# Attention into SwiGLU on one core: the third batch's score steps at closer slots, and the second batch's first P V in one step of four banks

## The chip, the cores and the metric

The kernel runs on one core of a Trainium2 chip. The metric is the device time of one execution in microseconds (us); several executions are timed and their median is taken. One more execution is profiled, and all rows and durations below come from it.

The core has TensorE (PE, with its weight loads listed apart as PEld), VectorE (DVE), ScalarE (ACT), GpSimd (POOL) and SyncE (SP), each with its own queue of instructions that it works through in order. Matmuls write into PSUM, which has eight banks of 128 x 512 fp32; ScalarE and VectorE read them from there.

## The reference

```python
# 8 batches, 8 heads, 1024 positions, head size 64, projection 64
k_proj = np.einsum('ks,bhsd->bhkd', E, k)
v_proj = np.einsum('ks,bhsd->bhkd', F, v)
scores = scale * np.matmul(q, k_proj.transpose(0, 1, 3, 2))
attn = softmax(scores)                       # over the 64 projected keys
attn_out = np.matmul(attn, v_proj)
x = attn_out.transpose(0, 2, 1, 3).reshape(8192, 512)
g = x @ w_gate                               # 512 x 1536
out = (silu(g) * (x @ w_val)) @ w_out        # 1536 x 512
```

Inputs and output are fp32, and the matmuls work in bf16.

## The kernel before

**Chunks and iterations.** A batch is cut into two halves ("ch") of 512 positions, which makes 16 chunks `c`. The feed-forward part of a chunk needs its attention output `xT[b, ch]` (four tiles of 128 features by 512 positions). The main loop runs over 16 x 12 = 192 iterations `t`; iteration t does feature block f = t mod 12 of chunk c = t div 12: four gate matmuls (`f_g`, line 493, PSUM tile `gps`), four value matmuls (`f_v`, line 499, tile `vps`), both of 512 columns. ScalarE takes Tanh of the gate (line 496), VectorE makes s and then the hidden tile `hT` (lines 503 and 508) from it and the value. "g" and "v" have two PSUM banks each, so a gate or value matmul group needs the bank of the group two before it to have been read.

The output matmuls of the chunk before (`f_m`, line 626; for chunk 0 `f_y`, line 514) are placed behind the value matmuls, by a table `late`. From chunk 1 on they are done in a form with seven half-size products instead of eight, for which GpSimd and VectorE make sums of hidden quarters (`hs`, line 569), and the parts are put together at lines 602 to 625 with the banks "y" and "z" (one each).

**Slots.** All attention work of the following batches is put by hand between these groups. Iteration t has the slots 2t (after its gate matmuls) and 2t + 1 (after its value matmuls and output matmuls). `put(s, fn, ...)` files a step under a slot, `run_slot(s)` calls what is there; this sets the order in which each engine's instructions are issued. Loads of a slot go first. `place(b)` (line 681) holds the slots of batch b; s0 = 48 (b - 1). Batches count from 0 in the code: the second batch is b = 1, the third is b = 2.

**The steps of one batch.**

- `u_TD` (line 327): a transposing DMA of the queries, issued by SP, one for each half.
- `u_KV`, `u_K1`, `u_V1`, `u_KT`: projections of k and v, and the block-diagonal `BD` that the scores are multiplied with. `VS` holds the projected values.
- `u_S` (line 343): one score step, four matmuls of 128 columns (line 353) into one "a" bank, and one Exp on ScalarE (line 357). A half has four, a batch eight (`sa[0]` to `sa[7]`).
- `u_R` (line 365) in the slot after it: sum and reciprocal on VectorE (lines 368 and 370).
- `u_N` (line 373) in the same slot: the product with the reciprocal on GpSimd (line 383), into `AAd`, a tile for one half.
- `u_AD` (line 335): the turn of a half, a transposing DMA from `AAd` to `AT` (line 337), issued by SP. It needs all four products of its half. For the third batch on it stands four slots behind the fourth and the eighth score step.
- `u_PVt` (line 419): P V of a half. Each group g does four matmuls of 64 x 64 (line 430) into two PSUM banks; then the banks are copied to `xT` by ScalarE (line 439), last group first. It waits for `AT`. The argument `gs` says which of the two groups, and `ats` from which pools each group's two banks come.

**Banks.** "a" has two banks. While the loop is in chunks 0 and 1, each request for "a" is served in rotation from three banks:

```python
if where == "a" and ring["wide"]:
    where = "aaz"[ring["n"] % 3]
    ring["n"] += 1
```

From chunk 2 on (slot 48) "a" means its own two banks.

**Queues.** SP issues all transposing DMAs and the stores of the output, in the order of the program. GpSimd issues the loads of k, v and q between its own products; for the fourth batch (b = 3) they stand at slots 76, 78, 80 and 82. The query turns of the fourth batch are put at slots 90 and 92. Up to eight banks, two `AT`, two `AAd` and two `qTd` tiles are shared by all batches.

Of the kernel before, what the change touches and what calls it, by code (L numbers as in the profile page):

```python
# [38 lines left out]
def kernel(  # L39
# [638 lines left out]
    def put(s, fn, *a):  # L678
        slots[s].append((fn, a))

    def place(b):
        s0 = 48 * (b - 1)
        if b == 1:
            put(22, u_TD, 1, 0)
            put(29, u_K1, 1)
            put(32, u_KT, 1)
            put(40, u_V1, 1)
            sa = (35, 36, 37, 38, 41, 42, 43, 44)
            put(41, u_AD, 1, 0)
            put(30, u_TD, 1, 1)  # L690
            put(47, u_AD, 1, 1)
            put(45, u_PVt, 1, 0, (0,), ("aa", "aa"))
            put(46, u_PVt, 1, 0, (1,), ("aa", "aa"))
        else:
            if b == 2:
                put(s0 + 10, u_KV, b)
            else:
                put(s0 + 8, u_KV, b, "kv", (0, H), "v")
            put(s0 + (13 if b == 2 else 11), u_KT, b)
            put(s0 + (9 if b == 2 else -6), u_TD, b, 0)  # L700
            put(s0 + (11 if b == 2 else -4), u_TD, b, 1)
            sa = [s0 + j for j in ((17, 22, 24, 27, 30, 33, 36, 39) if b == 2 else (14, 17, 20, 23, 26, 29, 32, 35))]
            put(sa[3] + 4, u_AD, b, 0)
            put(sa[7] + 4, u_AD, b, 1)
            put(s0 + 44, u_PVt, b, 0, (0, 1), ("aa", "yz"))
        for j in range(NJ):
            put(sa[j], u_S, b, j)
            put(sa[j] + 1, u_R, b, j)
            put(sa[j] + 1, u_N, b, j)
        put(s0 + (68 if b == 1 else 56), u_PVt, b, 1, (0, 1), ("aa", "yz"))  # L710
# [5 lines left out]
    with tc.manual_schedule():  # L716
# [129 lines left out]
        for b in range(1, B):  # L846
            place(b)
        for b in range(2, B):
            s0 = 48 * (b - 1) - (20 if b == 3 else 24)
# [71 lines left out]
```

## Time and profile before

| what | value |
| --- | --- |
| median of 3 runs | 549.01 us (548.2 to 549.5) |
| the profiled execution's own time | 548.17 us |
| its span in the profile | 546.4 us, so 1.77 us lie around it |
| granted TensorE clock, mean | 1.00 of full speed |
| busy: PE / DVE / POOL / ACT | 98% / 75% / 54% / 43% of the span |
| one iteration of the loop, third batch on | about 2.7 us (the k and v projections start at 159.06 and 223.91, 24 iterations apart) |
| score step: PE / ACT / DVE / POOL | 0.22 / 0.60 / 0.68 + 0.20 / 1.05 us |
| turn of `AAd` to `AT`, issue to landing (14) | least 4.3, median 13.7, greatest 19.7 us |
| third batch's score steps start on PE | 106.06, 113.23, 115.83, 119.96, 123.43, 128.21, 131.67, 135.80 us |
| third batch's turns issued by SP | 124.19 and 148.21 us |
| fourth batch's loads issued by GpSimd | k 122.15, v 124.10, q 129.22 and 131.40 us |
| P V: second batch / third batch | 77.35 and 78.66, 109.62 / 142.83, 158.43 us |

Times in the rows are counted from the start of the span. A matmul's end in the trace is modelled and overlaps the next one, so lengths on PE are best read from the start of one group to the start of the next: a group of four 512-column matmuls takes 0.86 us that way, though each is shown with 0.38. "idle before" in brackets is the time that the engine had nothing running in front of a row, with what released it. The share of busy time is an average; what a stage is limited by is read from the rows of that stage.

### The profile page before, as it was taken

To read this page: it belongs to the slowest core of one execution; us is meant where nothing else is said; L and a number is where in the kernel's file an instruction comes from. 1 tells how busy PE (TensorE), PEld (TensorE's weight loads), DVE (VectorE), ACT (ScalarE), POOL (GpSimd) and SP (SyncE) were. 2 spreads that over 40 slices of the span, in tenths; PEclk is the share of its full clock that TensorE was granted. 3 is DMA by queue.
4 is the path that set the end of the run, shared out by engine and by line. 5 is a ranking of instruction groups with operands and counts; after the bars stand their busy time and mean duration, and the time that the engine had idled before them with its cause. 6 is when DMAs were issued, how large, how long until landed. Compare 5 with 4: busy or idle time off the path is not lost.

```text
span 546.4 us, 9372 instructions
## 1 busy us (share of the span) xinstructions
PE 534.6 (98%) x3494; PEld 313.6 (57%) x3556; DVE 412.5 (75%) x697; ACT 233.2 (43%) x416; POOL 294.6 (54%) x364
## 2 busy tenths in 40 slices
PE   8999999999999999999999999999999999999997
PEld 4654445556555665566555665556655565556565
DVE  3787897779578886788777886787967888676884
ACT  3664443354444334444344444434344433443331
POOL 6952493466616854168641875338660665426162
PEclk9999999999999999999999999999999999999999
DMA  9999979919941499018990099612993133110013
GB/s 203 189 196 189 166 153 192 169 40 146 212 106 40 91 184 215 13 39 132 191 180 38 29 154 201 121 40 51 170 200 82 39 78 79 38 40 9 30 40 117
DMA packets 111630, 62.88 MB, mean 115 GB/s; under 512 B 65888, under 2 KB 102752, under 8 KB 111584
## 3 DMA queue, kind: packets, MB, share of 16 engines
q0 software_dynamic: 43952, 29.49, 38.0%
q1 hardware_dynamic: 66800, 31.20, 27.0%
q10 hardware_dynamic: 832, 1.57, 0.9%
q8 instruction: 28, 0.46, 0.4%
q14 instruction: 18, 0.15, 0.1%
HBM read 60.29 MB, written 16.78 MB: 141 GB/s over the span
## 4 chain that ended last, share of the span: by engine, by line
PE 84%; DMA 12%; POOL 2%; issue 1%; ACT 0%; DVE 0%; POOLq 0%; DVEq 0%; ACTq 0%
PE vps L484 26%; PE gps L484 26%; PE yps L586 24%; DMA qTd<-qb 3%; DMA AT<-AAd 3%; PE sc L353 2%; DMA qb<-in_q_dram 2%; PE kvp L163 2%; PE pv L430 2%; DMA Fraw<-in_F_dram 1%; PE yps L520 1%; DMA wv<-in_moe_w_val_dram 1%; POOL wv L127 0%; POOL AA L383 0%; POOL wg L127 0%
## 5 line engine op out<-in xcount | busy, mean ns | idle before, releaser
L496 ACT ACTIVATE th<-gps 128x512 f32<-128x512 f32 x191 | 114.3, 598 | 197.3 <-PE gps L484 177.9
L484 PE MATMUL vps<-xT,wv 128*128 128x512 bf16 (+1 forms) x754 | 195.3, 377 | 0.9
L484 PE MATMUL gps<-xT,wg 128*128 128x512 bf16 (+1 forms) x734 | 192.4, 377 | 1.3
L503 DVE SCALAR_TENSOR_TENSOR s<-th,gps 128x512 f32<-128x512 f32 x191 | 129.3, 677 | 61.3 <-ACT th L496 59.9
L508 DVE SCALAR_TENSOR_TENSOR hT<-s,vps 128x512 bf16<-128x512 f32 x192 | 132.0, 688 | 22.6 <-PE vps L484 2.5
L569 POOL TENSOR_TENSOR hs<-hT 128x256 bf16<-128x256 bf16 x180 | 120.4, 692 | 48.7 <-DVE hT L508 48.6
L484 PEld LDWEIGHTS <-wv 128*128 128x128 bf16 x776 | 73.1, 98 | 84.6 <-issue 6.5
L586 PEld LDWEIGHTS <-hs 128*128 128x128 bf16 x900 | 88.0, 98 | 34.7 <-issue 0.6
L484 PEld LDWEIGHTS <-wg 128*128 128x128 bf16 x776 | 73.9, 98 | 51.6 <-issue 0.4
L616 POOL TENSOR_TENSOR tt<-tt,ysb 128x512 f32<-128x512 f32 x28 | 35.6, 1271 | 111.4 <-DVE tt L615 111.4
L383 POOL TENSOR_TENSOR AAd<-ee,rr 128x512 bf16<-128x512 f32 x56 | 58.5, 1046 | 34.5 <-DVE rr L370 28.9
L586 PE MATMUL yps<-ws,hs 128*128 128x256 bf16 x540 | 68.6, 273 | 0.2 <-DVE ysb L653 0.2
L357 ACT ACTIVATE ee<-sc 128x512 f32<-128x512 f32 x64 | 37.9, 596 | 30.7 <-PE sc L353 29.4
L605 POOL TENSOR_TENSOR tt<-xs 128x256 f32<-128x256 f32 x30 | 29.6, 987 | 37.5 <-ACT xs L603 37.0
L586 PE MATMUL yps<-ws,hT 128*128 128x256 bf16 x360 | 48.8, 273 | 0.3
L586 PE MATMUL yps<-wo,hs 128*128 128x256 bf16 x360 | 48.6, 273 | 0.1
L368 DVE TENSOR_REDUCE zz<-ee 128x8 f32<-128x512 f32 x64 | 43.3, 677 | 5.6 <-ACT ee L357 5.4
L569 DVE TENSOR_TENSOR hs<-hT 128x1536 bf16<-128x1536 bf16 (+1 forms) x49 | 45.3, 929 | 0.1
L586 PEld LDWEIGHTS <-hT 128*128 128x128 bf16 x360 | 35.2, 98 | 16.0
L439 ACT CAST xT<-pv 128x512 bf16<-128x512 f32 x56 | 28.9, 601 | 2.3 <-PE pv L430 2.3
L603 ACT COPY xs<-yps 128x512 f32<-128x512 f32 x30 | 17.6, 587 | 27.9 <-PE yps L586 24.6
L610 ACT COPY ysb<-yps 128x512 f32<-128x512 f32 x30 | 17.6, 587 | 27.7 <-PE yps L586 22.9
(100 smaller groups left out, 306.5 us busy)
## 6 DMA issues: line engine op xcount, KB each, us to landing
out_dram<-ysb SPq DMA_DIRECT2D x28, 512.0 KB, 2.7
qb<-in_q_dram POOLq DMA_DIRECT2D x14, 512.0 KB, 18.6
kb<-in_k_dram POOLq DMA_DIRECT2D x7, 1024.0 KB, 10.9
vb<-in_v_dram POOLq DMA_DIRECT2D x7, 1024.0 KB, 15.8
wo<-in_moe_w_out_dram POOLq DMA_DIRECT2D x2, 768.0 KB, 21.5
out_dram<-ysb SPq DMA_DIRECT2D x6, 256.0 KB, 2.3
kraw<-in_k_dram ACTq DMA_DIRECT2D x2, 512.0 KB, 5.0
qb<-in_q_dram POOLq DMA_DIRECT2D x4, 256.0 KB, 7.8
```

Of the source, the lines that this page charges most:

```text
L357: nc.scalar.activation(out=e[:].rearrange("p h j k -> p (h j k)"), in_=ps[:].rearrange("p a k -> p (a k)"), func=AF.Exp, scale=scale,)
L368: nc.vector.reduce_sum(out=z[:], in_=e[:], axis=AX.X)
L383: eng.tensor_tensor(out=a.rearrange("p j h k -> p h j k"), in0=ee.pop((b, u))[:], in1=rr.pop((b, u))[:].unsqueeze(3).to_broadcast([P, 4, 2 ...
L439: nc.scalar.copy(out=xT[b, ch][:, kt, :], in_=ps[:])
L484: nc.tensor.matmul(out=ps[:, ts], lhsT=(wg, wv)[w][:, kt, f * P : (f + 1) * P], rhs=x[:, kt, ts], start=(kt == 0), stop=(kt == NKT - 1),)
L496: nc.scalar.activation(out=th[:], in_=ps[:], func=AF.Tanh, scale=0.5)
L503: nc.vector.scalar_tensor_tensor(out=s1[:], in0=th[:], scalar=1.0, in1=g[:], op0=ALU.add, op1=ALU.mult)
L508: nc.vector.scalar_tensor_tensor(out=hT[c][:, f, :], in0=s1[:], scalar=0.5, in1=ps[:], op0=ALU.mult, op1=ALU.mult)
L569: eng.tensor_tensor(out=hs[c, m][:, fs, :], in0=quarter(hT[c], *a)[:, fs], in1=quarter(hT[c], *b)[:, fs], op=op,)
L586: nc.tensor.matmul(out=ps, lhsT=lhsT, rhs=ws[m][:, f, :] if rhs is None else rhs, start=(start and f == 0), stop=(f == HF - 1), skip_group ...
L605: nc.gpsimd.tensor_tensor(out=t[:, 0], in0=xs[:, 0], in1=xs[:, 1], op=ALU.add)
L616: nc.gpsimd.tensor_tensor(out=t[:], in0=t[:], in1=yo[c, p][:, 1:3], op=ALU.subtract)
```

## The change

Two places of `place(b)` differ.

```diff
@@ place(b), b == 1
-            put(45, u_PVt, 1, 0, (0,), ("aa", "aa"))
-            put(46, u_PVt, 1, 0, (1,), ("aa", "aa"))
+            put(46, u_PVt, 1, 0, (0, 1), ("aa", "av"))
@@ place(b), b >= 2
-            sa = [s0 + j for j in ((17, 22, 24, 27, 30, 33, 36, 39) if b == 2 else (14, 17, 20, 23, 26, 29, 32, 35))]
+            sa = [s0 + j for j in ((17, 18, 22, 23, 27, 30, 33, 36) if b == 2 else (14, 17, 20, 23, 26, 29, 32, 35))]
             put(sa[3] + 4, u_AD, b, 0)
             put(sa[7] + 4, u_AD, b, 1)
```

In the second batch's first half, P V was done in two steps: group 0 at slot 45 (behind iteration 22's value and output matmuls) and group 1 at slot 46 (behind iteration 23's gate matmuls), each into two banks of the rotation and each followed by two copies. Now both groups are one step at slot 46: eight matmuls into four banks, three of the rotation and one of "v", then four copies. The rotation is advanced by three instead of four.

In the third batch (s0 = 48) the eight score steps go from slots 65, 70, 72, 75, 78, 81, 84, 87 to 65, 66, 70, 71, 75, 78, 81, 84, and their sums, reciprocals and products with them, each one slot behind. The turn of the first half goes from slot 79 to 75, that of the second half from 91 to 88, which is ahead of the fourth batch's query turn at slot 90 and not behind it any more. P V of the third batch stays at slots 92 and 104. All other batches and steps are as before.

## The prediction

> **What bounds the kernel now.** I read the page first: shares of the span by engine, then waits, chain, and the timeline around the slots that the change names.
>
> ```profile
> PE 534.6 (98%) x3494; PEld 313.6 (57%) x3556; DVE 412.5 (75%) x697; ACT 233.2 (43%) x416; POOL 294.6 (54%) x364
> ...
> PE pv L430 <- DMA AT<-AAd: 1.0, 1, 1.0
> ```
>
> TensorE (PE) is busy 98% of the span. Of all its named waits, one lies behind the start-up and is worth a microsecond: P V waits once for a transpose. So an edit pays if it shortens PE's own sequence or removes this wait. The chain of waits between 118 and 150 us shows the wait:
>
> ```profile
> 124.19 18.59 DMA AT<-AAd
> 142.78 0.04 issue
> 142.83 0.63 PE pv L430 x8
> ```
>
> It is the third batch's first half: the transpose is issued at 124.19, lands 18.59 us later, and P V (slot 92) starts at that moment. Next the timeline of PE at the second batch's P V (slots 45 and 46):
>
> ```profile
> 76.40 0.81 PE L520 MATMUL yps<-wo,hT 128*128 128x512 bf16 x3
> 77.35 0.41 PE L430 MATMUL pv<-AT,VS 64*64 64x512 bf16 x4
> 77.70 1.04 PE L484 MATMUL gps<-xT,wg 128*128 128x512 bf16 x4
> 78.66 0.71 PE L430 MATMUL pv<-AT,VS 64*64 64x512 bf16 x4
> 79.30 1.04 PE L484 MATMUL vps<-xT,wv 128*128 128x512 bf16 x4
> 80.18 1.89 PE L520 MATMUL yps<-wo,hT 128*128 128x512 bf16 x8
> 81.90 1.03 PE L484 MATMUL gps<-xT,wg 128*128 128x512 bf16 x4
> ```
>
> In the same stretch the weight loads (PEld) and ScalarE's copies, from the timeline of all engines:
>
> ```profile
> 77.84 1.07 ACT L439 CAST xT<-pv 128x512 bf16<-128x512 f32 x2 [1.24 <-PE pv L430]
> ...
> 78.66 0.11 PEld L430 LDWEIGHTS <-VS 64*64 64x64 bf16 x3 [0.42 <-issue]
> ...
> 78.97 0.10 PEld L430 LDWEIGHTS <-VS 64*64 64x64 bf16 x1 [0.20 <-issue]
> ```
>
> And slot 68, where the same function does both halves of its work in one step:
>
> ```profile
> 108.67 1.03 PE L484 MATMUL gps<-xT,wg 128*128 128x512 bf16 x4
> 109.62 0.63 PE L430 MATMUL pv<-AT,VS 64*64 64x512 bf16 x8
> 110.18 1.04 PE L484 MATMUL vps<-xT,wv 128*128 128x512 bf16 x3
> ...
> 110.30 2.06 ACT L439 CAST xT<-pv 128x512 bf16<-128x512 f32 x4
> ```
>
> Columns: start, duration, engine, line, operation. Durations overlap, so I count from start to start: four 512-wide matmuls take 0.86 us (the chain's pieces of four, and 81.90 to the next group at 82.77; single records are missing, so x3 stands for four too). The reader is to see the pause inside the second step (the fourth weight load comes at 78.97, as the first step's copies end at 77.84 + 1.07 = 78.91), and that eight matmuls in one step have no such pause.
>
> **Part 1, one step of four banks at slot 46.** Start to start, the first small step costs 77.70 - (76.40 + 0.86) = 0.44 us, the second 79.30 - (77.70 + 0.86) = 0.74 us, together 1.18. The single step at 109.62 costs 110.18 - (108.67 + 0.86) = 0.65 us. Gain: 0.53 us. Its two pieces: 0.74 - 0.44 = 0.30 us is the second step's wait for the first bank's copy (three banks in rotation, the fourth allocation meets the first again; the new fourth bank is one of "v"), and 1.18 - 0.30 - 0.65 = 0.23 us is one pair of changes between 128x128 and 64x64 matmuls. The Trainium skill, "TensorEngine Tiling (Array Packing)", Key Properties, says that a change of tiling mode drains TensorE. By that rule alone one step instead of two would be worth the 0.23 us and no more; the rows show 0.53, and I follow the rows.
>
> What the step has to meet. (a) Its "v" bank was last read by hT of two iterations earlier, long done; the value matmul of iteration 23 now takes the bank of iteration 22, whose hT runs 77.26 to 77.95. New times: gate 77.26, P V 78.21, value 78.77. Free by 0.8 us. (b) ScalarE: Tanh of iteration 23 starts 1.07 to 1.10 us after its gate, so 78.35, ends 78.95; four copies take 2.06, so the last ends at 81.0. The gate of the next chunk reads all four; PE arrives at 81.90 - 0.53 = 81.37. Cover 0.37 us. Were it gone, each microsecond of lateness costs one. The next readers of ScalarE's queue (a copy of y, then Tanh) had over a microsecond of idle time in front of them. (c) Transposed AT of this half was issued at 70.47, 4.7 us to landing: no issue. I take 0.53; bounds 0 (the copies late by all of it) and 0.60.
>
> **Part 2, scores at 17, 18, 22, 23, 27, 30, 33, 36 instead of 17, 22, 24, 27, 30, 33, 36, 39.** As sets, two positions change: the score step of slot 87 moves to 66 and that of 72 to 71; the other six positions stay and carry a different part. Nothing is added: eight score steps of 0.22 us on PE, eight Exp of 0.60, eight reductions (0.68 + 0.20) on VectorE (DVE), eight products of 1.05 on GpSimd (POOL). The first turn needs four products, so it now follows slot 72, not 76. Computed: PE is at -0.53 from part 1 and +0.22 from the extra score step, so the step of slot 71 ends at about 114.9, its Exp at 115.7. DVE reduces slot 70 till 116.65, slot 71 till 117.55; the product ends at 118.8. The turn is issued there, against 124.19: 5.4 us earlier. SP's only earlier entry is the output at 116.20, done in 0.4.
>
> What the turn then takes: this tile's times from issue to landing are 4.3 / 13.7 / 19.7 us (least, median, greatest). The short ones are those without loads beside them, and the DMA engines are idle from about 119.0 to 123.5 now, until the third load of k (issued at 122.15) begins. Near 124 is my estimate; even with 19.7 it is 138.5. P V wants it at 140.78 + 0.95 - 0.53 = 141.2 (0.95 is gate to P V at 108.67). So the wait is gone with 2.7 us left in the worst row. Its size, start to start: 142.83 - (140.78 + 0.95) = 1.10 us (the list's 1.0 counts from a modelled end). That is the second term; bounds 0 and 1.10.
>
> Costs of the move, each with its cover. PE runs 0.22 us later from slot 66 to 87, then it is returned. DVE: the reduction of slot 67 falls into the 0.90 us in which s waits for Tanh at 110.36; that of slot 72 puts 0.88 ahead of s of iteration 36, so its hT ends near 119.1, where value matmuls that want this bank start near 120.7; the next s finds its reduction already done. Without cover it would be 0.88 us. ScalarE: the Exp of slot 66 ends near 108.0, ahead of the copy that frees the "y" bank for P V of slot 68; that copy starts with PE (108.87 now) and not with Exp. POOL: one more product near 111, where it has 2.36 us idle before 113.20; the loads of k, v and q keep their places behind the same other work. The score step of slot 71 takes a bank whose copy ended by 112.4. All at nothing.
>
> SP's queue: the second turn (AD of slot 88, was 91) is now ahead of both query transposes of the fourth batch, where it stood between them. It can be issued at about 135.8 instead of 148.21, into the running loads. Behind it in the queue stand the two query transposes, issued at 145.16 and 151.34 now (the first waits for its load anyway), wanted by the scores at 168.8. An issue beside loads has held SP for up to 9.53 us: 135.8 + 9.5 = 145.3, no later than now. P V of the second half is at 158.43, new 156.8: it waits if this turn takes over 21 us.
>
> **Sum.** 546.40 (span) - 0.53 - 1.10 = 544.8; with the 1.77 us around it, 548.17 becomes 546.5. The profiled execution is the lowest of the runs shown (548.2, 549.0, 549.5); on their median 549.01 - 1.63 = 547.4. I predict the median.
>
> **Rivals.**
> A. Only the transpose wait goes; the four copies hold the next chunk's gate and return part 1. For it: ScalarE must do 2.06 us in a row with 0.37 to spare. Against: slot 68 runs the very same sequence in the time used. 549.0 - 1.1 = 547.9; with part of it, 547.4 to 547.9.
> B. Only part 1 is gained: the turn is held up on POOL or DVE, or lands behind the loads, and P V waits as before. 549.0 - 0.5 = 548.5. Against: 5.4 us of lead where 1.1 is needed.
> C. Slower: the second turn, now in the middle of the loads, lands after 156.8, and P V of slot 104 is the new wait, with all later work behind it. It decides from 21.0 us on; above 23.7 us both gains and 1.1 us more are gone: 550.1. The greatest of 14 turns is 19.7. For it: it is issued with 3 MB of loads in flight, as the 18.59 us turn was. Against: the loads' last packets are over near 147.6 now, and it can finish then.
> The skill's "SBUF — State Buffer", Who interferes with whom, speaks against more GpSimd work here: a DVE instruction with two SBUF inputs and a GpSimd one that reads SBUF block each other. The row agrees: hs on DVE takes 1.28 us at 123.71 beside a product, else 0.95. By that rule a moved product may cost DVE 0.33 us, and PE nothing as long as DVE's idle time stands; no such hs lies beside the two moved products.
>
> **Chances.** Forecast (both gains) 0.68, A 0.13, B 0.13, C and other losses 0.06. No change means within 0.2%, 1.1 us, which is about what a measurement of this kernel can tell. The forecast itself is 1.6 below the median and runs spread by about 0.7 to each side, so some of it falls within no change, as does most of B and half of A: faster 0.70, same 0.24, slower 0.06. Range: 546.2 (1.63 and 1.2 of spread to the lower side) to 548.6 (case B).
>
> **What would show it.** One group of eight P V matmuls near 78.2 with no pause in the weight loads; value matmuls 0.56 us behind; the next chunk's gate at 81.4 without ScalarE as its releaser. Turn issued near 119, landed before 130; no wait of P V for AT in the list; P V of slot 92 at 141.2 and everything after it 1.6 us earlier. Wrong if a wait of PE for AT appears at slot 104, or for a query transpose near 167, or if the copies end after 81.4.

## The result and the profile after

| | before | changed |
| --- | --- | --- |
| median (6 runs each) | 548.43 us (548.06 to 549.5) | 546.64 us (546.45 to 547.08) |
| ratio, 95% interval | | 0.9966 [0.9953, 0.9978] |
| profiled execution: own time / span | 548.17 / 546.4 us | 546.79 / 545.0 us |

The changed kernel is 1.79 us faster; the interval leaves 1.2 to 2.6 us. That is under 2%, but the whole interval lies beyond the 0.2% within which the prediction speaks of no change.

First the second batch's P V, in the timeline of PE, to be laid beside the rows from 76.40 to 81.90 of before:

```profile
77.52 1.03 PE L484 MATMUL gps<-xT,wg 128*128 128x512 bf16 x4
78.47 0.63 PE L430 MATMUL pv<-AT,VS 64*64 64x512 bf16 x8
79.03 1.04 PE L484 MATMUL vps<-xT,wv 128*128 128x512 bf16 x4
79.91 1.89 PE L520 MATMUL yps<-wo,hT 128*128 128x512 bf16 x8
81.63 1.03 PE L484 MATMUL gps<-xT,wg 128*128 128x512 bf16 x4
```

There is one group of eight. From the gate group's start to the value group's start there are 79.03 - 77.52 = 1.51 us, as at slot 68 before. The output group ahead of all this begins 0.25 us later than before (76.65 against 76.40: this execution's start-up was slower), while the gate of the next chunk comes 0.27 us earlier (81.63 against 81.90). Part 1 gave 0.25 + 0.27 = 0.52 us.

The timeline of all engines shows the cover, ScalarE's copies:

```profile
79.15 2.05 ACT L439 CAST xT<-pv 128x512 bf16<-128x512 f32 x4
```

They end at 81.20, the gate that reads them starts at 81.63. The cover is 0.43 us and holds.

The third batch's first turn, in SP's timeline and then with its time to landing in the DMA view of 119 to 120 us:

```profile
116.16 0.38 SPq L622 DMA_DIRECT2D out_dram<-ysb  x1
119.14 1.67 SPq L337 DMA_TRANSPOSE AT<-AAd  x1
132.55 0.37 SPq L622 DMA_DIRECT2D out_dram<-ysb  x1
136.33 5.49 SPq L337 DMA_TRANSPOSE AT<-AAd  x1
143.10 7.39 SPq L330 DMA_TRANSPOSE qTd<-qb  x2
```

```profile
AT<-AAd SPq DMA_TRANSPOSE x1, 4.2
```

It is issued 5 us earlier and lands after 4.2 us instead of 18.6, so at 123.3; P V needs it at 141.5. PE at slot 92 no longer waits. First the timeline of before, then that of the changed kernel:

```profile
140.78 1.03 PE L484 MATMUL gps<-xT,wg 128*128 128x512 bf16 x4
142.83 0.63 PE L430 MATMUL pv<-AT,VS 64*64 64x512 bf16 x8 [1.02 <-DMA AT<-AAd]
143.38 1.04 PE L484 MATMUL vps<-xT,wv 128*128 128x512 bf16 x3
```

```profile
140.51 1.03 PE L484 MATMUL gps<-xT,wg 128*128 128x512 bf16 x4
141.47 0.63 PE L430 MATMUL pv<-AT,VS 64*64 64x512 bf16 x8
142.03 1.04 PE L484 MATMUL vps<-xT,wv 128*128 128x512 bf16 x3
```

Gate to P V is 0.96 us, against 2.05 before (142.83 - 140.78): 1.09 us gained. On the way there the moved score steps cost PE nothing: the gate group at 140.51 is 0.27 us earlier than before (140.78), just as the gate of chunk 2 was (81.63 against 81.90). The value group stands at 142.03 against 143.38, 1.35 us earlier, and that is where it stays: the projections of the fourth batch start 1.36 us earlier (157.70 in the chain, 159.06 before), the span ends 1.4 us earlier. No later wait takes anything back. 0.52 + 1.09 less the 0.25 of the start-up makes 1.36.

### The profile page after: what moved, and what is told of

It is laid out like the page before. It is cut to its first block, busy times and chain, and to the rows that moved or that the text cites. A ratio compares the mean times of both kernels' runs of the same rounds, so it can differ in the third digit from the quotient of the medians.

```text
span 545.0 us, 9374 instructions
## 1 busy us (share of the span) xinstructions
PE 534.2 (98%) x3494; PEld 313.4 (58%) x3556; DVE 412.8 (76%) x697; ACT 232.8 (43%) x416; POOL 294.2 (54%) x364
## 4 chain that ended last, share of the span: by engine, by line
PE 88%; DMA 8%; POOL 2%; issue 1%; ACT 0%; DVE 0%; POOLq 0%; DVEq 0%; ACTq 0%
PE vps L484 28%; PE gps L484 27%; PE yps L586 25%; DMA qTd<-qb 3%; PE sc L353 3%; DMA qb<-in_q_dram 2%; PE kvp L163 2%; DMA Fraw<-in_F_dram 1%; PE pv L430 1%; PE yps L520 1%; DMA wv<-in_moe_w_val_dram 1%; POOL wv L127 0%; POOL AA L383 0%; POOL wg L127 0%; POOL qb L117 0%
```

## The experiments

All ran beside the kernel before on the same chip, in three sets, and medians are compared within a set. The kernel before took 548.42 us in the first (28 runs, e1 to e4), 548.32 in the second (26, e5 to e7) and 548.45 in the third (10, e8 to e10).

**e1: part 1 alone.**

```diff
-            put(45, u_PVt, 1, 0, (0,), ("aa", "aa"))
-            put(46, u_PVt, 1, 0, (1,), ("aa", "aa"))
+            put(46, u_PVt, 1, 0, (0, 1), ("aa", "av"))
```

> Part 1 alone (P V of the second batch's first half in one step at slot 46; scores and turns of the third batch as before). Theory (two independent terms): TensorE gains 0.53 us at slots 45 and 46 and the wait of P V for AT at slot 92 stays at 1.1 us, so about 0.5 us below the kernel before. Rival (the two parts work together, or the gain of part 1 is given back at the AT wait, which then grows by what PE arrives earlier): no change, with a wait of about 1.6 us.

Measured 548.01 us, ratio 0.9993 [0.9981, 1.0004]: 0.4 us below, not clear of no change by the time alone. The trace is clearer. The step has the form of the changed kernel (gate 77.52, P V 78.48, value 79.04), and the AT wait is still there:

```profile
140.52 1.03 PE L484 MATMUL gps<-xT,wg 128*128 128x512 bf16 x4
142.53 0.63 PE L430 MATMUL pv<-AT,VS 64*64 64x512 bf16 x8 [0.98 <-DMA AT<-AAd]
```

142.53 - 140.52 - 0.95 = 1.06 us, not 1.6. PE arrives earlier, but so does the whole chain of scores, products, turn and loads that PE sets going (turn issued at 123.93, 18.6 us to landing). The rival falls.

**e2: part 2 alone.**

```diff
-... (17, 22, 24, 27, 30, 33, 36, 39) if b == 2 ...
+... (17, 18, 22, 23, 27, 30, 33, 36) if b == 2 ...
```

> Part 2 alone (closer score steps and earlier turns; P V of the second batch's first half in two steps as before). Theory: the AT wait at slot 92 is gone, 1.1 us below the kernel before, with the pause in the second small P V step still there. Rival (the closer steps cost something on DVE, ScalarE or GpSimd that part 1 hides): less than 0.8 us below.

Measured 547.30 us, ratio 0.9979 [0.9969, 0.9989]: 1.1 us below, as expected. The interval leaves 0.6 to 1.7 us, so the time alone does not exclude the rival's 0.8; the trace does. The first turn is issued at 119.45 and takes 4.2 us; gate to P V at slot 92 is 141.78 - 140.83 = 0.95. And PE loses nothing between the two places: the gate of chunk 2 is 0.05 us later than in the kernel before (81.95 against 81.90), and the gate of slot 92 is too (140.83 against 140.78). Together e1 and e2 make 1.5 of the 1.8 us, within what such medians allow; the parts add up.

**e3: what part 1 is made of.** Two steps as before, and one letter changed:

```diff
-            put(46, u_PVt, 1, 0, (1,), ("aa", "aa"))
+            put(46, u_PVt, 1, 0, (1,), ("aa", "av"))
```

> The kernel before with one letter changed: the second small P V step at slot 46 takes its fourth bank from v and not from the rotation; still two steps. It splits part 1. Theory: the bank wait of 0.30 us goes (no pause before the fourth weight load of that step), the second pair of tiling changes stays: value matmuls 0.44 us behind the end of the gate group, 0.3 us below the kernel before, not to be told from no change by the time alone; the trace decides. Rival (the pause is not the bank): the pause stays and 0.74 us too.

Measured 548.33 us, ratio 0.9997 [0.9987, 1.0008]: nothing to be seen in the time. The weight loads in its timeline decide:

```profile
77.53 0.11 PEld L430 LDWEIGHTS <-VS 64*64 64x64 bf16 x4 [0.42 <-issue]
77.88 0.55 PEld L484 LDWEIGHTS <-wg 128*128 128x128 bf16 x4 [0.23 <-issue]
78.84 0.11 PEld L430 LDWEIGHTS <-VS 64*64 64x64 bf16 x4 [0.42 <-issue]
79.19 0.55 PEld L484 LDWEIGHTS <-wv 128*128 128x128 bf16 x4 [0.23 <-issue]
```

The second step's four loads now come together, with no pause before the fourth. Its price is 79.19 - (77.88 + 0.86) = 0.45 us, that of the first 0.44. So the pause was the bank, 0.29 us, and the remaining 0.45 + 0.44 - 0.65 = 0.24 us of part 1 is one pair of tiling changes. It is not the price of any step put in between: a score step, four matmuls of 128 columns in the 128x128 form, costs 0.22 us, which is what 512 columns take (0.86 / 4). The idle times of the loader at each entry (0.42) and exit (0.23) fit what the Trainium skill's "TensorEngine Tiling (Array Packing)", Key Properties, says of a change of mode: TensorE drains. The rows agree with the rule, but it would have found less than half of the gain; the loader's idle 0.65 us is also not its price to PE, which is 0.24.

**e4: the turns back in their old slots,** the rest as in the changed kernel.

```diff
-            put(sa[3] + 4, u_AD, b, 0)
-            put(sa[7] + 4, u_AD, b, 1)
+            put(s0 + 31 if b == 2 else sa[3] + 4, u_AD, b, 0)
+            put(s0 + 43 if b == 2 else sa[7] + 4, u_AD, b, 1)
```

> The changed kernel with only the turns of the third batch put back to slots 79 and 91; scores stay close, P V in one step. Theory: the turn is issued by SP as soon as the fourth product is done (near 119 us), whatever its slot, since no other entry of SP stands in between; same time as the changed kernel, 546.6. Rival (the slot of the turn is what counts): the turn is issued near 124 again, and P V waits 1 us at slot 92: 547.7.

Measured 546.99 us, 1.4 us below the kernel before, ratio 0.9965 [0.9951, 0.9979], close to the changed kernel's 0.9966. P V of slot 92 does not wait (gate 140.10, P V 141.06). SP's timeline:

```profile
118.73 1.67 SPq L337 DMA_TRANSPOSE AT<-AAd  x1
132.15 0.37 SPq L622 DMA_DIRECT2D out_dram<-ysb  x1
141.41 3.01 SPq L330 DMA_TRANSPOSE qTd<-qb  x1
144.51 1.90 SPq L337 DMA_TRANSPOSE AT<-AAd  x1
```

The turn is issued when its fourth product is done. Its slot only matters for its place in SP's queue, which for the first turn is the same; the second one waits behind a query turn again (144.51, not 136.33) and nobody notices, as P V of slot 104 comes at 156.67. It is the score steps that brought the gain.

**e5: the kernel before, with the fourth batch's loads put later** instead of the scores earlier. The second turn goes to slot 89, so that it does not stand behind a query turn.

```diff
-            s0 = 48 * (b - 1) - (20 if b == 3 else 24)
+            s0 = 48 * (b - 1) - (16 if b == 3 else 24)
...
-            put(sa[7] + 4, u_AD, b, 1)
+            put(sa[7] + (2 if b == 2 else 4), u_AD, b, 1)
```

> The kernel before with the loads of the fourth batch four slots later (80, 82, 84, 86), and the second turn of the third batch at slot 89, so that it does not stand behind a query transpose that waits for these loads. Scores, the first turn (slot 79) and both small P V steps as before. Theory (the turn lands late because the loads share the DMA engines with it): issued near 124 as before, it lands in 4 to 7 us, P V at slot 92 does not wait, 1.1 us below the kernel before. Rival (the late issue itself is the cause): it lands 15 us or more after its issue again and the wait stays.

Measured 547.39 us, ratio 0.9985 [0.9973, 0.9998]: 0.9 us below; the near end of the interval is only 0.1 us from no change, so the trace decides. The turn in SP's timeline, its time to landing in the DMA view of 123 to 125 us, and the k load in GpSimd's timeline:

```profile
123.91 1.69 SPq L337 DMA_TRANSPOSE AT<-AAd  x1
```

```profile
AT<-AAd SPq DMA_TRANSPOSE x1, 4.3
```

```profile
129.12 0.94 POOL L98 DMA_DIRECT2D kb<-in_k_dram  x1
```

The turn is issued 0.28 us from where it was, lands in 4.3 us, and the k load comes behind it. Gate to P V is 141.99 - 141.03 = 0.96, no wait. The late turn was slow because of the loads beside it, and not because it was late.

**e6: the cover taken away.**

```diff
-            put(46, u_PVt, 1, 0, (0, 1), ("aa", "av"))
+            put(47, u_PVt, 1, 0, (0, 1), ("aa", "av"))
```

> The changed kernel with the one-step P V of the second batch's first half at slot 47, right ahead of the gate group that reads its result, and not at 46. It takes away the cover of the four copies. Theory: P V start to last copy is 2.73 us, P V start to the next group 0.56 us, so the gate of chunk 2 waits about 2.2 us for ScalarE: 548.8, about as much above the changed kernel. Rival (the copies are hidden by something else, or the first copies suffice): under 1 us above it.

Measured 549.12 us, ratio 1.0022 [1.0012, 1.0033], 0.8 us above the kernel before. Against that less the changed kernel's 1.79 us it is 2.6 us more. PE's timeline:

```profile
81.31 0.63 PE L430 MATMUL pv<-AT,VS 64*64 64x512 bf16 x8
84.09 1.02 PE L484 MATMUL gps<-xT,wg 128*128 128x512 bf16 x4 [2.16 <-ACT xT L439]
```

2.78 us instead of 0.56: a wait of 2.2 us, as worked out. The two profiles differ by the same amount: the span is 2.5 us longer (547.5 against 545.0), of which 0.25 us lay ahead of this place (output group at 76.90 against 76.65). One slot too late turns the gain of the whole change into a loss; at slot 46 there are 0.43 us to spare.

**e7: half the lead.** Score steps at 17, 22, 23, 24, 27, 30, 33, 36.

```diff
-... (17, 18, 22, 23, 27, 30, 33, 36) if b == 2 ...
+... (17, 22, 23, 24, 27, 30, 33, 36) if b == 2 ...
```

> The changed kernel with less lead: third batch's score steps at 17, 22, 23, 24, 27, 30, 33, 36, so that the first turn follows the step of slot 72 and is issued near 121.5, just ahead of the fourth batch's k load, not near 119. Theory (what counts is to be in front of the loads): it lands in under 10 us, no wait at slot 92, same as the changed kernel within 0.2%. Rival (the lead of 5 us counts as such; a landing is 18 us when loads follow): it lands near 140 and P V has under 1.5 us left or waits.

Measured 547.05 us, ratio 0.9975 [0.9965, 0.9985], 1.3 us below the kernel before; whether it is as good as the changed kernel these intervals don't say. The profiled execution was its slowest (548.7 us), late from the start: its first query turn was issued at 42.78 and not 41.15. The rows at slot 92 are counted from one another and can be read all the same. SP issues the turn and GpSimd the k load:

```profile
122.57 1.69 SPq L337 DMA_TRANSPOSE AT<-AAd  x1
```

```profile
123.19 0.94 POOL L98 DMA_DIRECT2D kb<-in_k_dram  x1
```

Landing takes 7.7 us, and gate to P V is 143.35 - 142.40 = 0.95: what the theory says, and not the rival's landing near 140. With e2, e5 and the kernels before and after this makes a row by the distance of the turn from the issue of the k load:

| turn issued | issue to landing |
| --- | --- |
| 5.2 us before the k load (e5) | 4.3 us |
| 3.0 us before it (changed, e2) | 4.2 us |
| 0.6 us before it (e7) | 7.7 us |
| 2.0 us after it (before) | 18.6 us |

From the third line to the fourth are 2.6 us of distance and 10.9 us of landing time. The k load is not all that differs between these two: in the kernel before, the v load too was issued ahead of the turn (124.10 against 124.19), in e7 it came 3.5 us behind it (126.03). SP issues the turn and GpSimd the loads; the skill's "DMA: Bandwidth & Descriptors", section "Issuing engines are not separate DMA queues", says that DMAs of both run on the same 16 DMA engines and interleave. The table agrees in so far as a turn on SP's queue is slow when GpSimd's loads run beside it.

**e8, e9 and the changed kernel again.** In the profile after, the one PE wait for a transpose that is left is the second batch's first score step, at 59.94, behind a query turn that takes 18.7 us among the loads of the start. Two kernels try the same cure there.

```diff
-        put(20, load_v, 1)
+        put(25, load_v, 1)
```

> The changed kernel with the same idea used at the start: the second batch's load of v at slot 25 and not 20, so that fewer loads run beside the first query turn (issued at 41.15, 18.7 us to landing, and PE waits for it at 59.9 in the changed kernel's profile). Theory (a turn among loads is slow, wherever it is): the turn lands some microseconds sooner, the wait of 0.2 to 0.5 us goes: 0.3 us below the changed kernel. Rival (v then lands too late for its projection at slot 40, or its wait only moves): no gain, or slower, with a wait of PE for v near 68.

```diff
-            sa = (35, 36, 37, 38, 41, 42, 43, 44)
+            sa = (36, 37, 38, 39, 41, 42, 43, 44)
```

> The changed kernel with the second batch's first four score steps one slot later (36, 37, 38, 39 and not 35 to 38), so that PE has a gate group to do while the first query turn lands. Theory: the wait near 59.9 goes (0.2 to 0.5 us), and the first turn of this batch, then about 1 us later, still lands before P V at slot 46: 0.3 us below the changed kernel. Rival (the turn gets late): P V at slot 46 waits for AT, no gain.

> The changed kernel unaltered, beside the two others on one chip, as their measure. Theory and rivals alike: 1.4 to 1.9 us below the kernel before.

Measured: e8 546.76 us, 0.9969 [0.9956, 0.9981]; e9 546.40 us, 0.9966 [0.9953, 0.9978]; the changed kernel 546.72 us, 0.9969 [0.9957, 0.9981]. e8 brings nothing, and it has hardly tested its idea, as GpSimd's timeline shows:

```profile
42.84 0.94 POOL L117 DMA_DIRECT2D qb<-in_q_dram  x1
43.77 0.88 POOL L108 DMA_DIRECT2D vb<-in_v_dram  x1
```

GpSimd has no product between the two slots that would hold the load back, so v only changed places with the second load of q: v was issued at 43.77 and not at 42.31, q at 42.84 and not at 43.25. Both still run beside the turn, with k until 46.5 and the second load of the output weights until 57.1. The turn takes 17.7 us, one less; PE does not wait for it in this profile, but PE also comes 0.5 us later there (output group at 58.21 and not at 57.69). Whether a load of v that is really later would help stays open. In e9's profile the wait is gone, and P V at slot 46 doesn't wait either; its median is 0.3 us lower, and the intervals can't tell that from none. In the profile of e10 PE loses only 0.1 us at this place (output group at 57.50, eight matmuls of 0.216, first score at 59.35), where the first profile of the changed kernel lost 0.5 (57.69 to 59.94); the query turn was issued at 40.59 there, 0.56 us earlier. So this wait grows and shrinks with the start-up. None of the three is shown to be better than the others.

## Why the prediction was right

1. *Bound: PE's sequence and one wait.* Right. Each of the two terms moved everything behind it by its full size, and the end with it.
2. *Part 1, 0.53 us.* 0.52 in the trace, 0.4 in e1's median. Its two pieces, bank 0.30 and tiling 0.23, were measured apart in e3: 0.29 and 0.24.
3. *Copies end at 81.0 with 0.37 us of cover.* 81.20 with 0.43, in an execution 0.25 us late. e6 shows that the cover is needed, and its price.
4. *Part 2, turn at 118.8, landing near 124, wait of 1.10 us gone.* 119.14, 123.3, 1.09 us; e2's median 1.1 us. That the loads were what made the turn slow was only read from DMA idle time; e5 shows it.
5. *Costs at nothing.* They were: PE's lead of 0.27 us at chunk 2 is still 0.27 us at slot 92. On DVE the reduction of slot 67 used up most of the idle time, 0.90 us, down to the 0.29 us of this row in the timeline of the changed kernel:

```profile
110.31 0.69 DVE L503 SCALAR_TENSOR_TENSOR s<-th,gps 128x512 f32<-128x512 f32 x1 [0.29 <-ACT th L496]
```

   and hT of iteration 36 ends at 119.06 (said: near 119.1). PE did not notice.
6. *Second turn near 135.8, query turns not later than now.* 136.33, and 143.10 for the first of them. It landed in 11.4 us, 9 us before P V of slot 104 needs it. Rival C was far from its point of 21 us. The 3 MB of loads in flight that spoke for it were a misreading: when the turn of 18.59 us was issued, k and v were on their way, 2 MB (q was issued 5 and 7 us later), and at 136.33 it was v and both halves of q, also 2 MB, as k had landed at 133.0. And e4 shows that this order in SP's queue is worth nothing either way.
7. *Rivals A and B.* A needed the copies to be late, B the wait to stay; the rows show neither.
8. *Sum.* 1.63 us was forecast, 1.79 measured between the medians, 1.36 between the two profiles with a start-up that differs by 0.25. The predicted 547.4 us stood on a median of three runs, 549.01, which lay 0.6 above the median of six; the difference was right, the base was high.

## What to carry to other kernels

When the tensor engine is full, look for its few named waits and price them from start to start against the same step elsewhere in the trace; here two such prices, each with its own cause, added up. A short transfer issued behind big loads can take several times as long (18.6 us here at 2.0 us behind, 4.2 at 3.0 us ahead of them), so look at what is issued ahead of it, and not only at when it is wanted. And a step that is made bigger needs the time to drain its results: say which slot has it, as one slot later cost 2.2 us here.

## What had not been expected

The landing time of the turn goes from 7.7 to 18.6 us within 2.6 us of issue time (e7 and before), while 3.0 and 5.2 us of lead make no difference (4.2 and 4.3); four points do not show the shape between. And executions of one kernel differ by some tenths of a microsecond in the first 60 us: in two profiles of the changed kernel the first query turn was issued at 40.59 and 41.15, as its load landed, the first score step started at 59.35 and 59.94, and the spans are 544.5 and 545.0, as PE is full behind it. In e7's profile the turn came at 42.78, and there it was another thing: PE stood 1.35 us waiting for the load of the input E, then the granted clock was 0.82, 0.50 and 0.83 in the stretches of 2 us from 6 to 12 us (1.00 throughout in the profile after). The first scores on PE started at 12.69 and not at 10.82.
